# One tile's rounding ahead of another's copies, DRAM copies of x in three places, and the fourth group's tiles ahead of w1's maxima, in a fused FNet and MLP layer

## The chip, the core and the metric

The kernel runs on one core of a Trainium2 chip. The time is device microseconds from launch to end. Engines: TensorE (PE; PEld is its weight load), VectorE (DVE), ScalarE (ACT), GpSimd (POOL) and the queue of SyncE (SP), which issues most transfers. Each engine works through its own instructions in a fixed order.

## The reference

```python
def reference(A_x, A_dft_seq_re, A_dft_seq_im, A_dft_hid_re, A_dft_hid_im, B_x, B_w1, B_w2):
    ...
        a = jnp.einsum("bsd,ed->bse", x, dft_hid_re)
        b = jnp.einsum("bsd,ed->bse", x, dft_hid_im)
        y = jnp.einsum("ts,bse->bte", dft_seq_re, a) - jnp.einsum("ts,bse->bte", dft_seq_im, b)
    ...
        h = jnp.einsum("bsd,df->bsf", x, w1)
        h = jnp.maximum(h, zero)
        return jnp.einsum("bsf,fd->bsd", h, w2)
    x = A_x
    xn = _layernorm(x, axis=-1)
    return x + _A_ref(xn, A_dft_seq_re, A_dft_seq_im, A_dft_hid_re, A_dft_hid_im) + _B_ref(xn, B_w1, B_w2)
```

x is 2048 x 576, w1 is 576 x 4608, w2 is 4608 x 576, all float32. The result is x plus the real part of a two-sided Fourier transform of the normalized x plus a two-layer MLP of it.

## The kernel before

float32 products are made of float16 pairs: a value is scaled by a power of two and split into hi (ACT rounds it to float16) and lo (DVE takes the rest), and three matmuls, hi hi, hi lo and lo hi, make one product. The scales come from maxima over the weights: DVE's magnitude for w1 (max_w1), ACT's sum of absolute values for w2 (sum_w2), followed by a maximum over the partitions (power on POOL, or power_pe on PE and DVE in block 0, with its result in a tile named top).

x has 16 tiles of 128 rows, in four groups of four. stats takes the mean and the variance of a group's tiles on DVE and ends in r (the factor) and sh (the shift), four tiles at once. normalize (N) makes xn in float32 on DVE, or on ACT for tiles 10 and 11, and xs, the hi, on ACT. remainder (E) makes the lo, on POOL for tiles 1 to 11, on DVE for the others. transposes_dma (TD) lets POOL copy a piece and SP issue a DMA transpose into xT; the first four tiles are transposed by PE instead (transposes), and ACT copies them out of PSUM (copies).

The MLP runs in nine blocks b of 512 hidden columns. A step is a pair (b, g). mlp1 makes the four outputs of a step, each 128 hidden columns by the 512 rows of a group; mlp1_out applies the ReLU and makes h's hi and lo and four sums of them, from which mlp2 makes seven products by Strassen's scheme. Each product is 12 matmuls for a block of two. mlp2 has two PSUM tiles, so a product waits until the one two before it has been evicted: the first of an output by ACT (L583), the others by DVE (L586). In block 0 the results go into the acc tiles; POOL adds them to a DRAM tensor, spill, by a DMA that accumulates (L590). spill must hold x before that: copy_x(g) copies x of group g into it, DRAM to DRAM, by four transfers of 288 KB on SP.

At the start, stages are written out by hand, for tiles 0 to 11: that part runs from the loads of x to the first mlp2. Then a loop over the steps n runs mlp1 of step n and mlp2 of step n - 1. At n = 2 it also makes tiles 12 to 15 (the fourth group), while a list todo, emptied piece by piece by work(), prepares the weights of the next block: load_w1, max_w1, split_w1, then load_w2, sum_w2 and the splits of w2. w2's load for block 1 uses the two buffers named raw, so its second half waits until the second half of w1 is split.

The instructions of each engine are ordered by a scheduler. behind(key) and issue_after put what follows behind a named instruction of the same engine: "td" is the last transpose on SP, "add" the first eviction on DVE, ("sh", t) the last of a group's statistics, "pe" the last matmul of mlp2, "top" the maximum of power_pe. Where a key is not yet set, behind does nothing.

Of the kernel before, what the change touches and what calls it, by code (L numbers as in the profile page):

```python
# [13 lines left out]
AF = mybir.ActivationFunctionType  # L14
# [35 lines left out]
def kernel(  # L50
# [46 lines left out]

    def load_raw(key, src, shape):
        r = raws[key] = raw.tile(shape, F32, tag="raw", name="raw_" + "_".join(map(str, key)))
        order["raw"] = nc.sync.dma_start(r, src).ins  # L100

    def load_w1(b, i, parts=1):
        pool, tag = (raw, "raw") if b else (mlp, "stage")
# [4 lines left out]

    def load_w2(b, i):
        load_raw(("w2", b, i), w2[b, i], [P, 4, EH])  # L110
        if b == 1:
            copy_x(2 + i, "raw")


    def magnitude(dst, src):
# [82 lines left out]

        return tc.issue_after(order[key]) if key in order else nullcontext()

    def stats(ts, after=None):

        n = len(ts)
        mv = small.tile([P, n, 2], F32, tag=f"mv{n}", name=f"mv{ts[0]}")
        sts = [small.tile([P, 2, 6], F32, tag="st", name=f"st{t}", bufs=4) for t in ts]
        for t, st in zip(ts, sts):
            for j in range(2):
                with behind(after):
                    nc.vector.bn_stats(st[:, j, :], acc[t][:, j * EH : (j + 1) * EH])
                yield  # L210
        for i, st in enumerate(sts):
            order["stats"] = nc.vector.bn_aggr(mv[:, i], st.rearrange("p a b -> p (a b)")).ins
            yield
        r0, u, r, sh = (
            small.tile([P, n], F32, tag=f"{a}{n}", name=f"{a}_{ts[0]}") for a in ("r0", "u", "r", "sh")
        )
        m, v = mv[:, :, 0], mv[:, :, 1]
        stt = nc.vector.scalar_tensor_tensor
        order["root", ts[0]] = nc.scalar.activation(u, v, AF.Sqrt, bias=eps).ins
        nc.vector.reciprocal(r0, u)  # L220
        yield

        stt(u, v, EPS, r0, ALU.add, ALU.mult)
        yield
        nc.vector.tensor_tensor(u, u, r0, ALU.mult)
        yield
        nc.vector.tensor_scalar(u, u, -0.5 * SX, 1.5 * SX, ALU.mult, ALU.add)
        yield
        nc.vector.tensor_tensor(r, u, r0, ALU.mult)
        yield  # L230
        order["sh", ts[0]] = stt(sh, m, -1.0, r, ALU.mult, ALU.mult).ins
        for i, t in enumerate(ts):
            means[t], factors[t], shifts[t] = mv[:, i, 0:1], r[:, i : i + 1], sh[:, i : i + 1]

# [11 lines left out]
    def normalize(t, eng=nc.vector, after=None):  # L246
        stage = dbufs[t % 4]
        xn = xns[t] = stage[:, :D]

        xs = xss[t] = stage[:, D : 2 * D + P // 2].bitcast(F16)  # L250
        with behind(after):
            if eng is nc.scalar:
                nc.scalar.activation(xn, acc[t], AF.Identity, bias=shifts[t], scale=factors[t])
            else:
                eng.tensor_scalar(xn, acc[t], means[t], factors[t], ALU.subtract, ALU.mult)
            nc.scalar.activation(xs[:, :D], acc[t], AF.Identity, bias=shifts[t], scale=factors[t])

    def remainder(t, eng):
        xn, xs = xns[t], xss[t]
        eng.tensor_tensor(  # L260
            xs[:, D : D + REM], xn[:, KM * P :], xs[:, KM * P : D], ALU.subtract
        )
        eng.tensor_tensor(
            xs[:, D + REM : 2 * D], xn[:, : KM * P], xs[:, : KM * P], ALU.subtract
        )

    def transposes_dma(t, eng):

# [289 lines left out]
    def mlp2(b, g, n):  # L558

        qa, qb, first, row, col = PRODUCTS[n]
        if first:
            places[n] = ps2.tile([P, 2, 512], F32, tag="ps2", name=f"p2_{b}_{g}_{n}")[:, :, :EH]
        ps = places[PLACE[n]]
        for c in range(2):
            for i in range(NQ):
                h, w = hs[b, g, i], w2s[b, i]  # L570
                for j, (x, y) in enumerate(((0, 0), (0, 1), (1, 0))):
                    order["pe"] = nc.tensor.matmul(  # L572
                        ps[:, c], h[:, x, qa, c * P : (c + 1) * P], w[:, y, qb],
                        start=first and i == 0 and j == 0, stop=i == NQ - 1 and j == 2,
                        skip_group_check=not first,
                    ).ins
        if n in (0, 2, 3, 6):
            if b:
                o = sumbufs[sum_buffer(g, n)]
            else:  # L580
                o = accs[g].rearrange("p (h c) (j e) -> p h j c e", h=2, j=2)[:, row, col]
            sums[row, col] = o
            freed(nc.scalar.activation(o, ps, AF.Copy, scale=us[b]))  # L583
        else:
            o = sums[row, col]
            add = nc.vector.scalar_tensor_tensor(o, ps, us[b], o, ALU.mult, ALU.add)  # L586
            order["acc"] = order["vfree"] = add.ins
            order.setdefault("add", add.ins)
        if n not in (0, 2, 3):
            nc.gpsimd.dma_start(spill[g, row, col], o, accum_op=ALU.add)  # L590

# [2 lines left out]
    def max_w1(b, f):  # L594

        i, r = divmod(f, 2)
        if f == 0:
            mx["w1", b], sc["w1", b], pw["w1", b] = cell("mw1"), cell("sw1"), cell("pw1")
        if r == 0:
            mx["f", b] = cell("mf", 2)  # L600
        with behind("vfree" if b >= BB else "add" if b else ("sh", 1) if f > 1 else None):
            magnitude(mx["f", b][:, r : r + 1], raws["w1", b, i][:, r * KT : (r + 1) * KT])
        if r:
            if b:
                m = mx["w1", b][:, i : i + 1]
            else:
                m = mx["b", i] = small.tile([P, 1], BF16, tag=f"mb{i}", name=f"mb{b}_{i}")
            nc.vector.tensor_reduce(m, mx["f", b], AX.X, ALU.max)
# [39 lines left out]
        tt(a12, a12, a11, ALU.subtract)  # L648
        tt(r[:, 4], r[:, 4], r[:, 9], ALU.subtract)

    def sum_w2(b, i):

        if i == 0:
            mx["w2", b], sc["w2", b], pw["w2", b] = cell("mw2"), cell("tw2"), cell("pw2")
        if b:
            junk = mlp.tile([P, 5, GH], F32, tag="stage", name=f"j{b}_{i}")
            junk = junk.rearrange("p a b -> p (a b)")[:, : 4 * EH]
            junk = junk.rearrange("p (q e) -> p q e", e=EH)
        else:
            new_w2(b, i)  # L660
            junk = w2s[b, i][:, 0, :4]
        with behind("free" if b >= BB else None if b else ("root", 4)):
            nc.scalar.activation(
                junk, raws["w2", b, i], AF.Abs, scale=2.0**-10, accum_out=mx["w2", b][:, i : i + 1]
            )
# [72 lines left out]
    def prepare_w2(b):  # L738
        p = power_w2(b)
        steps = [long(lambda: sum_w2(b, 0))] + [lambda: None] * (b >= BB)  # L740
        steps += [
            long(lambda: (sum_w2(b, 1), b and next(p))),
            lambda: None,
            lambda: later(p) if b else next(p, None),
        ]
# [27 lines left out]
    for t in range(2 * TG, NT):  # L773
        load_x(t)

    def copy_x(g, key="td"):

        for row, col in itertools.product(range(2), range(2)):
            t = g * TG + row * 2
            src = x[t * P : (t + 2) * P, col * EH : (col + 1) * EH]  # L780
            with behind(key):
                nc.sync.dma_start(spill[g, row, col], src.rearrange("(c p) e -> p c e", p=P))

    warm = const.tile([P, 1], F32, name="warm")
    nc.scalar.activation(warm, eps, AF.Sqrt)

# [55 lines left out]
    tile_by(1, (3,), ps)  # L842
    weave(stats([4, 5, 6, 7]))
    copies(2, pt, ("root", 4))
    T(3)
    w = prepare_w2(0)
    w[0]()
    w[1]()
    tile_by(2, (0, 1, 2, 3), ps)
    for t in (4, 5, 6):  # L850
        N(t)
        E(t, GP)
        TD(t, GP)
    tile_by(3, (0, 1, 2, 3), ps)
    weave(stats([8, 9, 10, 11], ("sh", 4)))
    N(7, after=("root", 8))
    E(7, GP)
    TD(7, GP)
    w[3]()
    pq = ps2.tile([P, 2, 512], F32, tag="ps2", name="p1_0_1")  # L860
    qs = [pq[:, 0], pq[:, 1]]
    mlp1_out(0, 0, 0, *ps[:2], after="top")
    order["s0"] = order["s"]
    with behind("pm"):
        for t in (4, 5):
            tile_by(t, (0, 1), qs)
    for t in (8, 9):
        N(t, after="s4")
        E(t, GP)
        TD(t, GP)  # L870
    mlp1_out(0, 0, 1, *ps[2:])
    for t in (6, 7):
        tile_by(t, (0, 1), qs)
# [9 lines left out]
    for f in w[7:]:  # L883
        f()
    mlp1_out(0, 1, 1, *q2, after="w2")
    copy_x(0)
    mlp2(0, 0, 0)
    with behind("pe"):
        early = [mlp1(0, 2, 0), mlp1(0, 2, 1)]
# [102 lines left out]
    for n in range(2, len(steps)):  # L992
# [46 lines left out]
        for i in range(NF):  # L1039
            if n == 2:  # L1040
                ps.append(early.pop(0) if early else mlp1(b, g, i))
            else:
                mlp1_step(b, g, i, ps)
            if i % 2:
                mlp1_out(b, g, i // 2, *ps[i - 1 : i + 1], after="w2hi" if n == 2 else None)
            if i == (3 if n == 2 else 1):

                gates[n - 2] = order["s"], order["lo"]
            if n == 2:
                t = (g + 1) * TG + i  # L1050
                normalize(t)
                remainder(t, nc.vector)
                transposes_dma(t, nc.scalar)
                if i == 2:
                    todo += prepare_block(1)
                for _ in range(6):
                    work()
                continue
# [13 lines left out]
            if n > 3 and i % 2 and passes:  # L1072
                passes.pop(0)()
        if n == 2:
            copy_x(1)
            for q in range(7):
                mlp2(pb, pg, q)
    while todo:
# [229 lines left out]
```

## Time and profile before

| | us |
|---|---|
| median of three runs | 1260.19 (1258.29 to 1261.9) |
| the profiled execution | 1260.05, of which span 1258.3 |
| PE busy | 1231.6 |
| DVE busy | 1011.0 |
| ACT busy | 702.4 |
| POOL busy | 161.2 |

The granted TensorE clock of the profiled execution is 0.996 on average. In the profile a line such as L572 is a line of the kernel above. A row of the timeline shows the start, the length, engine, line, operation, output and inputs with their shapes, and how often in a row; the brackets hold the engine's idle time before it and what ended it. In a row of stretches, each engine's busy time is followed by its count of instructions.

### The profile page before, as it was taken

How to read it: one execution, taken by the hardware profiler on the slowest of the kernel's cores; microseconds unless marked ns; L12 is line 12 of the kernel's file. 1: busy time of each engine (PE TensorE's matmuls, PEld its weight loads, DVE VectorE, ACT ScalarE, POOL GpSimd, SP SyncE). 2: the span in 40 equal slices, each digit the busy share in tenths (PEclk: the TensorE clock that was granted, in tenths of full speed). 3: DMA queues.
4: the chain of work that ended last, by engine and by line, in shares of the span. 5: the costliest groups of instructions: out<-in, count | busy, mean ns of one | idle time of the engine just before them, and what ended most of it. 6: DMA issues, size and time to landing. Idle time of an engine off the chain costs nothing.

```text
span 1258.3 us, 25304 instructions
## 1 busy us (share of the span) xinstructions
PE 1231.6 (98%) x10269; PEld 983.0 (78%) x10269; DVE 1011.0 (80%) x1919; ACT 702.4 (56%) x1192; POOL 161.2 (13%) x207
## 2 busy tenths in 40 slices
PE   8888999999999999999999999999999999999998
PEld 7554656888888888888888888877777777777777
DVE  8997997878878787788788878556788888787885
ACT  5655466576676666676766756544553333333332
POOL 1521211111111111212121211100000000000000
PEclk9999999999999999999999999999999999999999
DMA  6787557565657575666666666640053435343420
GB/s 231 164 182 149 117 117 155 115 133 138 135 118 176 118 156 119 131 144 122 130 139 151 140 134 123 116 96 1 1 168 109 146 97 168 121 133 119 144 86 20
DMA packets 80901, 159.39 MB, mean 127 GB/s; under 512 B 22288, under 2 KB 41232, under 8 KB 80784
## 3 DMA queue, kind: packets, MB, share of 16 engines
q1 hardware_dynamic: 58000, 115.30, 28.6%
q0 software_dynamic: 22784, 42.48, 25.0%
q8 instruction: 80, 1.31, 0.5%
q14 instruction: 37, 0.30, 0.1%
HBM read 106.63 MB, written 51.90 MB: 126 GB/s over the span
## 4 chain that ended last, share of the span: by engine, by line
PE 78%; DVE 12%; ACT 1%; issue 1%; DMA 1%; POOL 0%; DVEq 0%; POOLq 0%; ACTq 0%
PE p L1240 26%; PE p L572 22%; PE bank L495 21%; PE pd L1121 8%; DVE w2s L186 2%; DMA raw_w<-in_w_dram 1%; PE p L339 1%; DVE dbuf L456 1%; DVE h L517 1%; DVE h L385 1%; DVE acc L441 1%; ACT w2s L185 0%; DVE sum L586 0%; DVE raw_w L697 0%; DVE dbuf L586 0%
## 5 line engine op out<-in xcount | busy, mean ns | idle before, releaser
L572 PE MATMUL p<-w2s,h 128*128 128x288 f16 x3024 | 410.0, 287 | 9.3 <-ACT acc L583 4.8
L572 PEld LDWEIGHTS <-h 128*128 128x128 f16 x3024 | 296.1, 98 | 86.6 <-issue 10.4
L1240 PE MATMUL p<-R,cs 128*128 128x288 f16 x2688 | 329.4, 286 | 0.0
L1240 PEld LDWEIGHTS <-cs 128*128 128x128 f16 x2688 | 263.0, 98 | 66.3
L185 ACT ACTIVATE cs<-c,sc_c 128x1024 f16<-128x1024 f32 x112 | 125.2, 1144 | 196.7 <-DVE c L1183 72.3
L186 DVE SCALAR_TENSOR_TENSOR cs<-c,sc_c,cs 128x1024 f16<-128x1024 f32 x112 | 141.0, 1282 | 54.7 <-ACT cs L185 54.7
L495 PEld LDWEIGHTS <-w1buf 128*128 128x128 f16 x1600 | 156.5, 98 | 22.8 <-issue 1.7
L495 PEld LDWEIGHTS <-dbuf 128*128 128x128 f16 x1200 | 117.4, 98 | 17.2 <-issue 1.5
L495 PE MATMUL bank<-xT,w1buf 128*128 128x256 f16 x832 | 109.8, 273 | 0.0
L1121 PE MATMUL pd<-dbuf,xT 128*128 128x288 f16 x832 | 103.8, 286 | 0.0
L495 PE MATMUL bank<-acc,w1buf 128*128 128x256 f16 x768 | 102.1, 273 | 1.0 <-DVE acc L525 0.9
L1121 PEld LDWEIGHTS <-xT 128*128 128x128 f16 x832 | 80.8, 98 | 22.0 <-issue 1.9
L517 DVE TENSOR_TENSOR h<-s,h 128x1024 f16<-128x1024 f32 x56 | 68.5, 1224 | 33.8 <-ACT h L514 33.6
L590 POOL DMA_DIRECT2D spill<-dbuf x70 | 61.0, 875 | 234.7 <-DVE dbuf L586 203.8
L502 ACT ACTIVATE h<-acc 128x256 f16<-128x256 f32 x112 | 45.9, 411 | 76.0 <-DVE acc L525 73.3
L495 PE MATMUL bank<-xT,dbuf 128*128 128x256 f16 x624 | 82.3, 273 | 0.0
L514 ACT ACTIVATE h<-s 128x1024 f16<-128x1024 f32 x56 | 59.1, 1056 | 34.5 <-DVE s L509 33.5
L495 PE MATMUL bank<-acc,dbuf 128*128 128x256 f16 x576 | 76.6, 273 | 0.9 <-DVE acc L525 0.9
L1246 DVE SCALAR_TENSOR_TENSOR o<-p,us_c,o 128x288 f32<-128x288 f32 x112 | 57.5, 514 | 12.6 <-PE p L1240 11.9
L984 ACT ACTIVATE f<-f 128x1024 f32<-128x1024 f32 x64 | 67.0, 1046 | 0.1
L503 DVE SCALAR_TENSOR_TENSOR h<-acc,h 128x256 f16<-128x256 f32 x112 | 47.3, 422 | 20.4 <-ACT h L502 20.4
L590 POOL DMA_DIRECT2D spill<-sum x42 | 36.3, 864 | 193.6 <-DVE sum L586 168.5
(161 smaller groups left out, 1537.3 us busy)
## 6 DMA issues: line engine op xcount, KB each, us to landing
spill<-dbuf POOLq DMA_DIRECT2D x70, 288.0 KB, 5.2
f<-in_cre_dram SPq DMA_DIRECT2D x32, 512.0 KB, 5.8
f<-in_cim_dram SPq DMA_DIRECT2D x32, 512.0 KB, 5.3
c<-in_cre_dram SPq DMA_DIRECT2D x32, 512.0 KB, 4.1
c<-in_cim_dram SPq DMA_DIRECT2D x32, 512.0 KB, 5.1
spill<-sum POOLq DMA_DIRECT2D x42, 288.0 KB, 4.9
raw_w<-in_w_dram SPq DMA_DIRECT2D x17, 640.0 KB, 6.0
raw_w<-in_w_dram SPq DMA_DIRECT2D x18, 576.0 KB, 5.0
```

Source lines behind the costliest of these rows:

```text
L185: nc.scalar.activation(hi, src, AF.Copy, scale=s).ins,
L186: nc.vector.scalar_tensor_tensor(lo, src, s, hi, ALU.mult, ALU.subtract).ins,
L495: nc.tensor.matmul(ps, l, r, start=first and m == 0, stop=m == len(todo) - 1, skip_group_check=not first,)
L503: stt(lo, src, 0.0, hi, ALU.max, ALU.subtract)
L514: order["s"] = nc.scalar.activation(hi_s, st[:, 1:], AF.Copy).ins
L517: order["lo"] = nc.vector.tensor_tensor(lo_s, st[:, 1:], hi_s, ALU.subtract).ins
L572: order["pe"] = nc.tensor.matmul(ps[:, c], h[:, x, qa, c * P : (c + 1) * P], w[:, y, qb], start=first and i == 0 and j == 0, stop=i == NQ ...
L590: nc.gpsimd.dma_start(spill[g, row, col], o, accum_op=ALU.add)
L984: nc.scalar.activation(f, f, AF.Abs, scale=2.0**-10, accum_out=sums_c[:, n, q : q + 1])
L1121: nc.tensor.matmul(ps[j], xT[g][:, kx, c * P : (c + 1) * P], dsp[j][:, hl, k], start=(t % 2 == 0 and n == 0), stop=(t % 2 == 1 and n == le ...
L1240: nc.tensor.matmul(ps, w[:, a, k], r[:, c, rq], start=first and k == 0 and j == 0, stop=k == HK - 1 and j == 2, skip_group_check=not first,)
L1246: order["o"] = nc.vector.scalar_tensor_tensor(o, ps, us["c"][:, n : n + 1], o, ALU.mult, ALU.add).ins
```

## The change

- copy_x of groups 0 and 1 is called just behind the loads of x, that of group 2 where group 0's was, and that of group 3 where group 1's was. load_w2 no longer issues copies for groups 2 and 3.
- Tile 4's normalize, remainder and transpose are written ahead of tile 3's copies, tile 5's ahead of the second sum over w2 (behind tile 5's hi on ACT).
- Tiles 6 and 7 come behind group 2's square root; the last two statistics of group 2 stand behind power_pe's maximum (the new argument late) and are woven in later; tile 8 follows them directly.
- In the loop's step n = 2, a tile of the fourth group is normalized, split and transposed ahead of the outputs of a pair (mlp1_out) instead of behind them.
- max_w1 of block 1 stands behind ("sh", 12), the fourth group's last statistic, instead of behind "add", the first eviction.
- The first output of step n = 3 (mlp1_step) stands behind the last matmul of mlp2.

```diff
     def load_w2(b, i):
         load_raw(("w2", b, i), w2[b, i], [P, 4, EH])
-        if b == 1:
-            copy_x(2 + i, "raw")
...
-    def stats(ts, after=None):
+    def stats(ts, after=None, late=None):
...
-        nc.vector.tensor_tensor(r, u, r0, ALU.mult)
+        with behind(late):
+            nc.vector.tensor_tensor(r, u, r0, ALU.mult)
         yield
-        order["sh", ts[0]] = stt(sh, m, -1.0, r, ALU.mult, ALU.mult).ins
+        with behind(late):
+            order["sh", ts[0]] = stt(sh, m, -1.0, r, ALU.mult, ALU.mult).ins
...
-            order.setdefault("add", add.ins)
...
-        with behind("vfree" if b >= BB else "add" if b else ("sh", 1) if f > 1 else None):
+        with behind("vfree" if b >= BB else ("sh", 12) if b else ("sh", 1) if f > 1 else None):
             magnitude(mx["f", b][:, r : r + 1], raws["w1", b, i][:, r * KT : (r + 1) * KT])
...
-    def copy_x(g, key="td"):
+    def copy_x(g):
...
-            with behind(key):
+            with behind("td"):
                 nc.sync.dma_start(spill[g, row, col], src.rearrange("(c p) e -> p c e", p=P))
 
+    copy_x(0)
+    copy_x(1)
...
     copies(2, pt, ("root", 4))
-    T(3)
     w = prepare_w2(0)
     w[0]()
-    w[1]()
+    N(4)
+    E(4, GP)
+    TD(4, GP)
+    copies(3, transposes(3), ("N", 4))
+    N(5)
+    E(5, GP)
+    TD(5, GP)
+    w[1](("N", 5))
     tile_by(2, (0, 1, 2, 3), ps)
-    for t in (4, 5, 6):
-        N(t)
+    tile_by(3, (0, 1, 2, 3), ps)
+    rest = stats([8, 9, 10, 11], ("sh", 4), "top")
+    for _ in range(3 * TG + 4):
+        next(rest)
+    for t in (6, 7):
+        N(t, after=("root", 8))
         E(t, GP)
         TD(t, GP)
-    tile_by(3, (0, 1, 2, 3), ps)
-    weave(stats([8, 9, 10, 11], ("sh", 4)))
-    N(7, after=("root", 8))
-    E(7, GP)
-    TD(7, GP)
     w[3]()
+    weave(rest)
+    N(8)
+    E(8, GP)
+    TD(8, GP)
...
-    for t in (8, 9):
-        N(t, after="s4")
-        E(t, GP)
-        TD(t, GP)
+    N(9, after="s4")
+    E(9, GP)
+    TD(9, GP)
...
-    copy_x(0)
+    copy_x(2)
...
-                mlp1_step(b, g, i, ps)
-            if i % 2:
-                mlp1_out(b, g, i // 2, *ps[i - 1 : i + 1], after="w2hi" if n == 2 else None)
-            if i == (3 if n == 2 else 1):
-
-                gates[n - 2] = order["s"], order["lo"]
+                with behind("pe" if n == 3 and i == 0 else None):
+                    mlp1_step(b, g, i, ps)
             if n == 2:
                 t = (g + 1) * TG + i
                 normalize(t)
                 remainder(t, nc.vector)
                 transposes_dma(t, nc.scalar)
+            if i % 2:
+                mlp1_out(b, g, i // 2, *ps[i - 1 : i + 1], after="w2hi" if n == 2 else None)
+            if i == (3 if n == 2 else 1):
+
+                gates[n - 2] = order["s"], order["lo"]
+            if n == 2:
                 if i == 2:
...
         if n == 2:
-            copy_x(1)
+            copy_x(3)
```

More of the change, by code (lines that the diff above doesn't have):

```diff
@@ L99, in load_raw @@
         r = raws[key] = raw.tile(shape, F32, tag="raw", name="raw_" + "_".join(map(str, key)))
-        order["raw"] = nc.sync.dma_start(r, src).ins
+        nc.sync.dma_start(r, src)
     def load_w1(b, i, parts=1):
@@ L255, in normalize @@
                 eng.tensor_scalar(xn, acc[t], means[t], factors[t], ALU.subtract, ALU.mult)
-            nc.scalar.activation(xs[:, :D], acc[t], AF.Identity, bias=shifts[t], scale=factors[t])
+            order["N", t] = nc.scalar.activation(
+                xs[:, :D], acc[t], AF.Identity, bias=shifts[t], scale=factors[t]
+            ).ins
     def remainder(t, eng):
@@ L262, in remainder @@
         )
-        eng.tensor_tensor(
+        order["E", t] = eng.tensor_tensor(
             xs[:, D + REM : 2 * D], xn[:, : KM * P], xs[:, : KM * P], ALU.subtract
-        )
+        ).ins
     def transposes_dma(t, eng):
@@ L649, in sums_w1, with sum_w2 @@
         tt(r[:, 4], r[:, 4], r[:, 9], ALU.subtract)
-    def sum_w2(b, i):
+    def sum_w2(b, i, after=("root", 4)):
         if i == 0:
@@ L661, in sum_w2 @@
             junk = w2s[b, i][:, 0, :4]
-        with behind("free" if b >= BB else None if b else ("root", 4)):
+        with behind("free" if b >= BB else None if b else after):
             nc.scalar.activation(
@@ L741, in prepare_w2 @@
         steps += [
-            long(lambda: (sum_w2(b, 1), b and next(p))),
+            long(lambda *a: (sum_w2(b, 1, *a), b and next(p))),
             lambda: None,
@@ L1042 @@
             else:
-                mlp1_step(b, g, i, ps)
+                with behind("pe" if n == 3 and i == 0 else None):
+                    mlp1_step(b, g, i, ps)
+            if n == 2:
+                t = (g + 1) * TG + i
+                normalize(t)
+                remainder(t, nc.vector)
+                transposes_dma(t, nc.scalar)
             if i % 2:
@@ L1049 @@
             if n == 2:
[L1050 to L1053, printed above, removed]
                 if i == 2:
```

## The prediction

> **What bounds the kernel now.** I read the page's busy line first, then stretches of the first 126 us, then TensorE's instructions in order of time, then the chain of waits.
>
> ```profile
> span 1258.3 us, 25304 instructions
> PE 1231.6 (98%) x10269; PEld 983.0 (78%) x10269; DVE 1011.0 (80%) x1919; ACT 702.4 (56%) x1192; POOL 161.2 (13%) x207
> ...
> 23.00:31.50 8.50, 8.15 (x146) 7.98 (x144) 7.96 (x28) 7.52 (x14) 3.73 (x6) 1.00 0.01 2
> 25.84:47.57 21.73, 18.70 (x249) 15.85 (x247) 21.52 (x52) 17.48 (x29) 15.92 (x23) 0.92 0.60 101
> 47.57:93.05 45.48, 39.61 (x261) 25.20 (x260) 44.42 (x101) 24.85 (x42) 11.20 (x12) 1.00 0.81 182
> 98.17:105.81 7.64, 5.28 (x34) 3.12 (x32) 0.00 (x1) 1.83 (x4) 0.36 (x1) 1.00 1.14 276
> 200.00:807.00 607.00, 604.52 (x5211) 509.57 (x5210) 483.88 (x1061) 406.68 (x797) 106.59 (x137) 1.00 0.65 135
> ```
>
> In the last five rows the columns are the stretch, its length, the busy time of PE, PEld, DVE, ACT and POOL, the granted clock, the DMA share and GB/s. The whole program leaves PE 1258.3 - 1231.6 = 26.7 us idle. From 200 to 807 us it loses 2.5 us in 607; there PE is the bound, and the change adds and removes no matmul. So whatever it is worth lies in the first 130 us or so. There DVE is the bound: busy 21.52 of 21.73 us and 44.42 of 45.48, up to the end of the split of w1's second half of block 1 at 93.05. Then DVE stands still for 7.64 us. DMA does nothing from 23 to 31.5 (share 0.01) and is full from 98 to 106 (1.14).
>
> TensorE in that time (start, length, instructions, and in brackets the idle time before and who ended it):
>
> ```profile
> 25.64 6.42 PE L339 MATMUL p<-xT,w1buf 128*128 128x128 f16 x112
> 35.16 0.16 PE L168 MATMUL pm<-top,ones 1*128 1x2 bf16 x1 [2.90 <-DVE top L165]
> 35.45 13.75 PE L339 MATMUL p<-xT,w1buf 128*128 128x128 f16 x140
> 49.04 1.63 PE L572 MATMUL p<-w2s,h 128*128 128x288 f16 x12
> 52.59 6.20 PE L339 MATMUL p<-xT,w1buf 128*128 128x512 f16 x28 [1.91 <-DMA xT<-dbuf]
> 58.62 8.98 PE L572 MATMUL p<-w2s,h 128*128 128x288 f16 x72
> 73.49 3.10 PE L572 MATMUL p<-w2s,h 128*128 128x288 f16 x24
> ...
> 91.16 3.10 PE L572 MATMUL p<-w2s,h 128*128 128x288 f16 x24
> ...
> 106.92 4.52 PE L572 MATMUL p<-w2s,h 128*128 128x288 f16 x24 [3.47 <-ACT acc L583]
> 115.25 1.02 PE L572 MATMUL p<-w2s,h 128*128 128x288 f16 x7 [1.00 <-DVE acc L586]
> ```
>
> At 91.16 the first output of group 3 is whole; from there PE runs 12.3 us without a gap, to 106.92 - 3.47 = 103.45. The gaps at 35, 52, 107 and 115 are the stalls that the change can reach. Only the last two stand behind the DVE-bound stretch; an earlier gap that closes buys nothing unless DVE also gets through its list sooner.
>
> **The wait at 107.** The chain of waits (start, length, what), the instructions of ACT and SP, and the page's DMA issues:
>
> ```profile
> 93.07 10.83 DMA raw_w<-in_w_dram
> 105.81 0.17 DVE half L126
> ...
> 103.98 1.16 ACT L663 ACTIVATE j<-raw_w 128x1152 f32<-128x1152 f32 x1 [7.57 <-DMA raw_w<-in_w_dram]
> 106.14 1.36 ACT L583 ACTIVATE acc<-p,c_ub 128x576 f32<-128x576 f32 x2
> 85.69 4.05 SPq L782 DMA_DIRECT2D spill<-in_x_dram  x4
> 93.45 4.07 SPq L782 DMA_DIRECT2D spill<-in_x_dram  x4
> raw_w<-in_w_dram SPq DMA_DIRECT2D x18, 576.0 KB, 5.0
> 106.44:109.85 3.41, 2.93 (x13) 1.87 (x13) 3.41 (x12) 1.30 (x3) 0.00 (x0) 0.50 0.18 62
> ```
>
> The second load of w2 of block 1 takes 10.83 us, against 5.0 for the median of 18 such loads. ACT stands in L663 (the sum over that load), and behind it on ACT waits the eviction L583 that PE needs; on DVE, L126 waits for POOL's maximum over that sum. Four copies of x leave SP just ahead of that load and four just behind it. After the gap the granted clock is 0.50 for 3.41 us: the 24 matmuls take 4.52 us instead of 3.10.
>
> **Part 1: the copies of x.** Sixteen copies of 288 KB stay sixteen. Groups 0 and 1 go behind the loads of x on SP and run from some 22.5 us, when DMA is idle. One stretch in which almost nothing but copies runs gives the rate:
>
> ```profile
> 54.00:56.00 2.00, 2.00 (x11) 0.88 (x9) 2.00 (x3) 1.05 (x2) 0.00 (x0) 1.00 0.83 251
> 31.79 18.62 SPq L277 DMA_TRANSPOSE xT<-dbuf  x8
> ```
>
> 8 x 288 KB = 2.36 MB at 251 GB/s is 9.4 us, so to about 32. Before, the first transpose left at 31.79, so DMA was free; now the transposes of tiles 4 and 5 share the queue with the last copies. This costs nothing as long as PE waits for L168 anyway; without that cover it is up to 2 us at 33. Group 2 takes the place of group 0, group 3 that of group 1, so around the two loads of w2 only group 3 is left, ahead of the first one. With eight copies (9.4 us of DMA) taken out of 85 to 106, the load should take about the 5.0 us of its median; the additions to spill that POOL issues are still there, so the bounds are 5.0 and 10.83. I take 5.0: landing at 98.1 instead of 103.9, 5.8 earlier. ACT's L663 and POOL then release DVE's L126 at about 100, which is when DVE gets there (93.05 to 98.17, and its list is unchanged); of DVE's 7.64 us some 2 remain. PE's gap of 3.47 goes, with it the slow clock (4.52 - 3.10 = 1.42), and the 1.00 at 115, since DVE's eviction moves with L126. Sum: -5.9 us, bounds -5.9 and 0. Next late is DVE: it has no more slack than these 2 us.
>
> **Part 2: the head (tile 4's hi, the maximum ahead of two statistics).**
>
> ```profile
> 28.92 2.39 ACT L256 ACTIVATE dbuf<-acc,sh,r 128x576 f16<-128x576 f32 x3
> 29.88 0.30 POOL L260 TENSOR_TENSOR dbuf<-dbuf 128x64 f16<-128x64 f32 x1 [4.77 <-ACT dbuf L256]
> 33.61 1.15 POOL L263 TENSOR_TENSOR dbuf<-dbuf 128x512 f16<-128x512 f32 x1
> 33.70 1.08 DVE L231 SCALAR_TENSOR_TENSOR sh<-mv,r 128x4 f32<-128x4 f32 x1
> 34.70 0.41 DVE L165 TENSOR_REDUCE top<-pm 1x2 bf16<-1x256 f32 x1
> 31.34:34.76 3.42, 0.92 (x15) 0.72 (x13) 3.25 (x9) 2.22 (x6) 3.42 (x7) 1.00 0.53 97
> ```
>
> ACT makes tile 4's hi ahead of tile 3's two copies and of the second sum over w2, so about 2.3 us sooner; POOL and the transpose follow. DVE takes top ahead of r and sh, which saves L231's 1.08 and r's short instruction, which I put at 0.2 to 0.3: PE's L168 moves from 35.16 to about 33.8. The clock is 0.92 over 25.84 to 47.57 because it halves after the gap; with 1.6 us of gap instead of 2.90 that may go. PE would be through its 140 matmuls at 46.3 instead of 49.04.
>
> That is not a gain yet. mlp2(0, 0, 0) also needs w2's first lo parts from DVE, and DVE now has r, sh, tile 8's xn and one subtraction of w2 ahead of them, four instructions more. I put its start between PE's 46.3 and the old 49.0. Then come the transposes of tiles 10 and 11: their hi stands on ACT behind w2's split and h's sums, which wait for DVE's scale. I get tile 11's xT, for which PE waited until 52.59, between 51 and 53.5. DVE's list is the same length, so at 57 it is where it was: I take 0 for the head, bounds -1.5 and +1.5.
>
> **Part 3: fourth group's tiles ahead of w1's maxima and of a pair's outputs.** DVE's 44.42 us from 47.57 to 93.05 stay what they are; only the order changes. Three rows show the order's price:
>
> ```profile
> 59.97 1.06 ACT L392 ACTIVATE h<-s 128x1024 f16<-128x1024 f32 x1 [3.52 <-DVE s L390]
> 60.30 0.82 DVE L586 SCALAR_TENSOR_TENSOR acc<-p,c_ub,acc 128x576 f32<-128x576 f32 x1 [0.36 <-PE p L572]
> 61.76 1.22 DVE L393 TENSOR_TENSOR h<-s,h 128x1024 f16<-128x1024 f32 x1
> ```
>
> Before, DVE evicts the second product (L586) and takes a maximum while ACT makes h's hi; now L393 stands ahead of L586 and the maxima wait for ("sh", 12). DVE then idles until ACT is done: 59.97 + 1.06 + 1.22 + 0.82 = 63.1 for L586's end instead of 61.1. PE's third set of 12 of the row at 58.62 (at 58.62 + 2 x 8.98 / 6 = 61.6) waits for that bank. The two sets ahead of it can run sooner than before, so PE idles there for some 3.5 us, and what follows is 63.1 - 61.6 = 1.5 later, less the 0.4 of two matmuls of the next step that now stand in the gap. The fourth group's transposes are out sooner, but mlp2(0, 1, .) is then paced by DVE's evictions behind the tiles' work and h's, and mlp1_step(0, 3, 0), put behind the pair's last matmul, follows only then. I get the first output of group 3 at 92.3 instead of 91.2: +1.1, the split of w1 and so the load's issue still at 93. Bounds: -1.5 (the transposes' lead of some 2 us carries through) and +3.
>
> **Sum**, against the profiled execution's 1260.05 us (span 1258.3 and 1.75 around it; the median of the runs is 1260.19): -5.9 + 0 + 1.1 = -4.8, so 1255.2.
>
> **Rivals.**
>
> *Clock.* PE's new gap ahead of the bank is 3.5 us. The clock halved after 31.34 to 34.76, with 0.92 us of work in it, and after the gap of 3.47 at 107. If it halves here too, 24 matmuls cost 1.4 more, and a second time while mlp2(0, 1, .) waits for its evictions, about 1.0: -4.8 + 2.4 = -2.4, so 1257.6. The Trainium skill (TensorE: Matmul & The Clock Gate, What's actually happening) has the clock fall only after a whole idle window of some 3.4 us in a free-running grid. By that rule a gap of this length would often pass, and the time is 1255.2; the row of 31.34 speaks against it, since that stretch was not idle throughout.
>
> *The load is no faster.* POOL's additions to spill run in the same time. If they, not the copies, hold the load, part 1 is worth nothing: +1.1, so 1261.2, or near 1260 with half of the effect of the copies ahead of the first load. Against it: the loads at other times have additions around them too and take 5.0.
>
> *Slower: POOL and DVE hold each other.* L231 takes 1.08 us beside POOL's L263 and ends with it, where L165, which reads PSUM, takes 0.41. Eight such POOL instructions (tiles 4 to 11) now meet another part of DVE's list: r, sh and w2's scale instead of statistics. At 1.15 each they can hold DVE 9.2 us; if about half of that did so before, 4.7 more. Tiles 10 and 11 and all behind slip by it, and with part 3's upper bound the first output of group 3 is 4.7 + 3 = 7.7 late. Part 1's 5.9 goes against that: +1.8. The gaps are then long enough for the clock to fall twice, 2.4 as above: +4.2, so 1264.3. It decides once that output is more than 5.9 late. The Trainium skill (SBUF — State Buffer, Who interferes with whom) says that whichever of the two starts first keeps the shared ports for its whole instruction. By that rule the order of starts, which the change shifts, decides each one; the trace agrees in the row of L231.
>
> *More.* The head's gain carries through (-1.5) and the transposes' lead too (-1.5 instead of +1.1): 1260.05 - 5.9 - 3.0 = 1251.2.
>
> **How the numbers follow.** Forecast 0.45; clock 0.2; load no faster 0.12; slower 0.13; more 0.10. 0.3% of 1260 is 3.8 us, about what a measurement of this kernel can tell from no change. Faster by more: the forecast without its upper tail (0.40) and "more" (0.10), 0.50. Within: the rest of the forecast, clock and load, 0.37. Slower: 0.13. The forecast's own range is 1253 to 1257.5; the range that holds 8 in 10 reaches "more" below and the load's case above: 1251 to 1261.5.
>
> **What would show it.** The load of w2 lands within 6 us of its issue, and PE has no gap at ACT's L583 near 100; DVE's idle time ahead of the scale of w2 is under 3 us instead of 7.6. L168 starts near 33.8. A new PE gap of 3 us or more stands near 60 to 63 and ends with DVE's eviction. DVE's end of the split of w1 is at 92 to 94.5. From 200 us on nothing differs. The prediction is wrong if that load still takes 9 us, if w1's split ends after 96, or if PE's gaps before 93 grow by more than 3 us.

## The result, and the profile after

| | before | after |
|---|---|---|
| median of five runs, us | 1260.19 (1258.29 to 1261.9) | 1254.26 (1254.06 to 1254.48) |
| profiled execution, us | 1260.05, span 1258.3 | 1254.06, span 1252.3 |

The ratio is 0.9953, 95% interval 0.9938 to 0.9967: 5.9 us less, against the 4.8 of the forecast and inside its range. The line numbers differ from kernel to kernel; in this one mlp1's matmuls are L341, mlp2's L574, ACT's eviction L585, DVE's L588, h's lo L395, the split L184, top L163, the sum over w2 L664.

The profiled executions don't start alike: the first matmuls of mlp1 stand at 11.50 us here, at 12.20 before and between 11.93 and 12.86 in the runs below. So the same work can stand up to 1.4 us apart in two profiles for that alone; "on before's scale" below means with that difference taken off.

The busy line of the changed kernel's page:

```profile
span 1252.3 us, 25300 instructions
PE 1229.2 (98%) x10269; PEld 980.5 (78%) x10269; DVE 1010.4 (81%) x1919; ACT 702.3 (56%) x1192; POOL 159.2 (13%) x207
```

1252.3 - 1229.2 leaves PE 23.1 us idle instead of 26.7: of the 6.0 us, 3.6 are idle time and 2.4 busy time. The profile has three stretches of 3.41 us at half the clock before and one now, and matmuls in such a stretch take longer. Stretches of the changed kernel (stretch, length, busy time of PE, PEld, DVE, ACT, POOL, granted clock, DMA share, GB/s):

```profile
47.57:93.05 45.48, 37.59 (x236) 23.76 (x237) 42.31 (x96) 24.12 (x41) 9.97 (x10) 0.96 0.86 177
98.17:105.81 7.64, 7.64 (x53) 5.01 (x52) 5.64 (x15) 4.58 (x7) 0.38 (x2) 1.00 0.33 45
130.00:200.00 70.00, 68.77 (x437) 41.43 (x435) 66.79 (x133) 44.33 (x76) 12.09 (x14) 1.00 0.60 124
200.00:807.00 607.00, 604.40 (x5220) 510.30 (x5219) 483.35 (x1061) 405.05 (x794) 108.01 (x138) 1.00 0.65 135
```

The last row is that of before within 0.1 us of PE's time, and behind it PE idles 3.4 us to the end (3.6 before): nothing differs from 200 us on. From 130 to 200 us PE is busy 68.77 us instead of 67.51, so 1.3 us of the gain lie behind the 130 us to which the prediction confined it. In the second row, which was the stall, PE is now busy all 7.64 us (5.28 before) and the DMA share is 0.33 instead of 1.14. The first row is worse than before: PE is busy 2 us less there, at a lower clock, and DVE, which was busy 44.42 us, now idles 3.2. TensorE in order of time shows where:

```profile
33.20 0.16 PE L166 MATMUL pm<-top,ones 1*128 1x2 bf16 x1 [1.64 <-DVE top L163]
33.29 12.47 PE L341 MATMUL p<-xT,w1buf 128*128 128x128 f16 x140
45.59 1.63 PE L574 MATMUL p<-w2s,h 128*128 128x288 f16 x12
49.47 6.20 PE L341 MATMUL p<-xT,w1buf 128*128 128x512 f16 x28 [2.25 <-DMA xT<-dbuf]
55.51 3.10 PE L574 MATMUL p<-w2s,h 128*128 128x288 f16 x24
...
61.44 7.71 PE L574 MATMUL p<-w2s,h 128*128 128x288 f16 x48 [2.39 <-DVE acc L588]
68.98 5.78 PE L341 MATMUL p<-xT,w1buf 128*128 128x512 f16 x26
...
91.77 3.10 PE L574 MATMUL p<-w2s,h 128*128 128x288 f16 x24
...
103.90 3.26 PE L574 MATMUL p<-w2s,h 128*128 128x288 f16 x24
...
110.76 1.63 PE L574 MATMUL p<-w2s,h 128*128 128x288 f16 x12 [0.79 <-DVE acc L588]
```

PE starts mlp2(0, 0, 0) at 45.59 instead of 49.04, 3.45 us ahead, and still leads by 58.62 - 55.51 = 3.1 at the next set. Then the new gap at 61 and a half clock behind it (48 matmuls take 7.71 us, where two runs of 24 take 2 x 3.10) eat the lead and more: the row at 68.98 was at 67.44. At 103.90 the gap of 3.47 is gone, and PE is 3.0 ahead again. Of each of these leads 0.7 is the earlier start.

The chain of waits and DVE's timeline of the changed kernel:

```profile
92.97 6.39 DMA raw_w<-in_w_dram
101.27 0.17 DVE half L124
```

```profile
59.43 1.22 DVE L395 TENSOR_TENSOR h<-s,h 128x1024 f16<-128x1024 f32 x1 [1.12 <-ACT h L394]
60.57 0.81 DVE L588 SCALAR_TENSOR_TENSOR acc<-p,c_ub,acc 128x576 f32<-128x576 f32 x1
...
91.26 1.68 DVE L184 SCALAR_TENSOR_TENSOR dbuf<-raw_w,c_sw,dbuf 128x640 f16<-128x640 f32 x2
...
101.27 0.17 DVE L124 TENSOR_SCALAR half<-top 128x2 f32<-128x2 f32 x1 [2.00 <-POOL top L121]
```

The load is issued at 92.97, where it was at 93.07 (w1's split ends at 91.26 + 1.68 = 92.94), and lands after 6.39 us instead of 10.83. DVE waits 2.00 us for the maximum over it. And DVE stands still for 1.12 us at 58 because h's lo, which must wait for ACT, is ahead of the eviction that PE needs; before, the eviction was first.

### The profile page after: what moved, and what is told of

The parts are those of the page before. It is cut to its first block, busy times and chain, and to the rows that moved or that the text cites. A ratio compares the mean times of both kernels' runs of the same rounds, so it can differ in the third digit from the quotient of the medians.

```text
span 1252.3 us, 25300 instructions
## 1 busy us (share of the span) xinstructions
PE 1229.2 (98%) x10269; PEld 980.5 (78%) x10269; DVE 1010.4 (81%) x1919; ACT 702.3 (56%) x1192; POOL 159.2 (13%) x207
## 4 chain that ended last, share of the span: by engine, by line
PE 78%; DVE 12%; ACT 2%; issue 2%; DMA 1%; POOL 0%; DVEq 0%; POOLq 0%; ACTq 0%
PE p L1253 26%; PE p L574 21%; PE bank L497 21%; PE pd L1134 8%; DVE w2s L184 2%; DMA raw_w<-in_w_dram 1%; PE p L341 1%; DVE dbuf L458 1%; DVE h L387 1%; DVE acc L443 1%; DVE h L519 1%; ACT w2s L183 1%; DVE dbuf L588 0%; DVE raw_w L698 0%; DVE raw_w L696 0%
## 5 line engine op out<-in xcount | busy, mean ns | idle before, releaser
L574 PE MATMUL p<-w2s,h 128*128 128x288 f16 x3024 | 410.4, 287 | 9.1 <-DVE acc L588 5.1
L574 PEld LDWEIGHTS <-h 128*128 128x128 f16 x3024 | 296.2, 98 | 86.4 <-issue 10.0
L184 DVE SCALAR_TENSOR_TENSOR cs<-c,sc_c,cs 128x1024 f16<-128x1024 f32 x112 | 141.0, 1282 | 54.4 <-ACT cs L183 54.4
L519 DVE TENSOR_TENSOR h<-s,h 128x1024 f16<-128x1024 f32 x56 | 68.5, 1223 | 33.9 <-ACT h L516 33.6
L585 ACT ACTIVATE dbuf<-p,c_ub 128x576 f32<-128x576 f32 x70 | 51.1, 732 | 16.5 <-PE p L574 16.2
```

The costliest lines, as they stand in the source:

```text
L184: nc.vector.scalar_tensor_tensor(lo, src, s, hi, ALU.mult, ALU.subtract).ins,
L519: order["lo"] = nc.vector.tensor_tensor(lo_s, st[:, 1:], hi_s, ALU.subtract).ins
L574: order["pe"] = nc.tensor.matmul(ps[:, c], h[:, x, qa, c * P : (c + 1) * P], w[:, y, qb], start=first and i == 0 and j == 0, stop=i == NQ ...
```

## The experiments

I call the three parts of the change the copies, the head and the group (part 3). Four kernels leave parts out. Times are medians; each ratio is to the kernel before run on the same chip (1259.25 to 1259.6 us, and 1260.19 for all three parts). The rows come from four chips, so rows are compared by their ratios.

| parts | us | ratio, 95% interval |
|---|---|---|
| copies | 1253.47 | 0.9954, 0.9940 to 0.9968 |
| head | 1256.65 | 0.9977, 0.9968 to 0.9986 |
| group | 1256.75 | 0.9977, 0.9968 to 0.9986 |
| copies, head | 1257.28 | 0.9979, 0.9970 to 0.9988 |
| copies, group | 1253.19 | 0.9950, 0.9938 to 0.9963 |
| head, group | 1254.98 | 0.9965, 0.9952 to 0.9978 |
| all three | 1254.26 | 0.9953, 0.9938 to 0.9967 |
| all three, lo behind the eviction | 1252.65 | 0.9945, 0.9932 to 0.9959 |
| copies, head, lo behind the eviction | 1252.13 | 0.9942, 0.9929 to 0.9954 |

The parts don't add: the three alone sum to 5.8 + 3.0 + 2.9 = 11.7 us, and together they give 5.9. The whole change (0.9953) is not set apart from the copies alone (0.9954).

**The copies alone** (the kernel before with)

```diff
-        if b == 1:
-            copy_x(2 + i, "raw")
...
+    copy_x(0)
+    copy_x(1)
     warm = const.tile([P, 1], F32, name="warm")
```

and groups 2 and 3 at the old places of 0 and 1.

> The kernel before with the copies of x alone moved (groups 0 and 1 behind the loads of x, 2 and 3 in the old places of 0 and 1). Theory (the copies carry the gain, 5 to 6 us, and the new order costs about 1): 1254 to 1255.5, the second load of w2 of block 1 lands within 6.5 us, DVE idles under 3 us ahead of w2's scale, no PE gap at ACT's eviction near 105. Rival (POOL's additions to spill hold that load, and the gain comes from the order of the engines' work): 1259 to 1261, and the load still takes 9 us or more.

1253.47, half a microsecond better than the theory's range. The chain of waits of this run:

```profile
94.80 5.56 DMA raw_w<-in_w_dram
```

The load takes 5.56 us, and PE's gaps from 93 to 126 us sum to 0.43 us instead of 4.83. The time has fallen by part 1's term of 5.9; the last pair of runs below shows that not all of it is this wait.

**The change without the copies** (copy_x of groups 0 to 3 back at the places of before).

> The changed kernel with the copies of x at their old places. Theory: 1260 to 1262, the load of w2 takes 9 us or more, PE has the gap of 3 us again, and DVE still ends the split of w1 at 92 to 94. Rival (order): 1254 to 1256.

1254.98: the theory missed, and the rival (order) has the time. The chain of waits and PE of this run:

```profile
93.19 7.20 DMA raw_w<-in_w_dram
```

```profile
106.56 1.63 PE L576 MATMUL p<-w2s,h 128*128 128x288 f16 x12 [0.20 <-ACT acc L587]
```

With all sixteen copies at their old places the load lands after 7.20 us instead of 10.83, and the gap at 107 is 0.20 us. What differs ahead of it is POOL's issue of the additions to spill; first the kernel before, then this run:

```profile
89.98 3.30 POOL L590 DMA_DIRECT2D spill<-acc  x3 [3.02 <-DMA spill<-in_x_dram]
```

```profile
85.89 1.11 POOL L594 DMA_DIRECT2D spill<-acc  x1 [1.16 <-DVE dbuf L456]
88.34 1.08 POOL L594 DMA_DIRECT2D spill<-acc  x1 [1.34 <-DVE half L126]
91.03 1.08 POOL L594 DMA_DIRECT2D spill<-acc  x1 [1.61 <-ACT acc L587]
```

Before, three additions leave in a bunch from 89.98 to 93.28, just ahead of the load at 93.07; the row puts their wait down to a copy of x. Here the outputs come sooner and the additions are spread. The bunch by itself does not slow the load: with the four copies ahead of the load moved away it stands there too, and the load takes 6.30 us (the last pair of runs below). Beside those copies it does go with the slow load: 10.83, 9.77 and 10.78 us with the bunch (before, the head alone, the copies behind moved), 7.20 and 7.55 without (here, the group alone). But in the last two the load is also issued 8.6 us behind the first of the four copies instead of some 7.5, so there was more time for the copies to drain. No run separates the two.

**The change without the group** (the loop of n = 2 and 3 and max_w1's key as before).

> The changed kernel without its third part: the fourth group's tiles behind a pair's outputs, w1's maxima behind the first eviction, the first output of step 3 not put behind mlp2. Theory (the order costs about 1, most of it the PE gap ahead of the bank at 61 and the slow clock behind it): 1252.5 to 1254, no PE gap of more than 1 us between 57 and 66. Rival (the fourth group's lead is what saves the stalls at 161 and 181 and more): 1255 to 1257.

1257.28: a miss, and 0.3 above the rival's range. DVE and then PE of this run:

```profile
60.04 1.23 DVE L395 TENSOR_TENSOR h<-s,h 128x1024 f16<-128x1024 f32 x1 [1.12 <-ACT h L394]
61.18 0.81 DVE L588 SCALAR_TENSOR_TENSOR acc<-p,c_ub,acc 128x576 f32<-128x576 f32 x1
```

```profile
62.04 7.60 PE L574 MATMUL p<-w2s,h 128*128 128x288 f16 x48 [2.38 <-DVE acc L588]
...
85.10 0.38 PE L341 MATMUL p<-xT,w1buf 128*128 128x512 f16 x1 [2.98 <-DVE dbuf L184]
```

The order lo, eviction and the gap behind it are there without part 3, which the forecast had made their cause. A second gap of 2.98 follows at 85, and w1's split ends at 93.95 + 1.68 = 95.6. The rival is right in this much: from 130 to 200 us PE idles 2.58 us here, 2.49 before and 1.23 with the whole change. The five kernels that have the whole group idle 1.1 to 1.2 us there, all others 1.5 to 2.6.

**The change without the head.**

> The changed kernel without its second part: tile 4's hi behind tile 3's copies, the maximum behind both statistics, tiles 6 to 8 as before. Theory (PE's 3 us at the head are waited away before DVE's evictions): 1253.5 to 1255.5. Rival (the head's 3.1 us carry through): 1257 to 1258.

1253.19, 0.3 below the theory's range; the rival missed. DVE's timeline of this run has the eviction first, and PE no gap there:

```profile
60.64 0.82 DVE L584 SCALAR_TENSOR_TENSOR acc<-p,c_ub,acc 128x576 f32<-128x576 f32 x1 [0.16 <-PE p L570]
61.60 1.23 DVE L391 TENSOR_TENSOR h<-s,h 128x1024 f16<-128x1024 f32 x1
```

Of all kernels here that keep mlp1_out whole, those with both copies and head have the lo ahead, and no others. Why the scheduler's order turns round just there is not shown.

**The lo behind the eviction**, in the changed kernel: the last line of mlp1_out becomes a function that is called later.

```diff
-    mlp1_out(0, 1, 1, *q2, after="w2")
+    lows = mlp1_out(0, 1, 1, *q2, after="w2", late=True)
...
     with behind("m1"):
         mlp2(0, 0, 1)
+    with behind("acc"):
+        lows()
```

> The changed kernel, with the lo of h's sums of the second group's second pair put behind DVE's first eviction of mlp2(0, 0, .) instead of ahead of it. Theory (the gap of 2.39 us at 61 and the half clock behind it are what the head costs): that eviction ends by 60.0 instead of 61.4, the gap falls under 1.2 us, the clock isn't halved at 62, and the time is 1252.5 to 1253.6, as low as without the head. Rival (DVE's list sets the pace up to the split of w1 at 93, so a gap of PE ahead of that buys nothing): the gap closes all the same, w1's split ends at 92.5 to 93.3 as now, and the time stays at 1254.0 to 1254.6.

1252.65, as the theory had it; the eviction ends at 60.7, which is 59.7 with the 1.0 us taken off by which this profile starts later than that of the changed kernel. PE of this run:

```profile
50.51 7.89 PE L341 MATMUL p<-xT,w1buf 128*128 128x512 f16 x28 [2.26 <-DMA xT<-dbuf]
58.24 8.98 PE L580 MATMUL p<-w2s,h 128*128 128x288 f16 x72
```

The gap at 61 is gone and 72 matmuls run through in 8.98 us. The load's issue moves from 92.97 to 91.78 in spite of that later start, so the rival (DVE's list alone sets the pace) doesn't hold. The clock fell all the same, at another gap (below). The two intervals overlap; the next use of the same edit is plainer.

**The same edit without the group** (copies and head; the same diff).

> The changed kernel without part 3 (the kernel of 1257.28 us), and again with the lo of h's sums behind DVE's first eviction of mlp2(0, 0, .). Theory (with copies and head together, that one order of two DVE instructions and the half clock behind its gap is most of what the head cost): gap at 62 under 0.8 us, w1's split ends by 94.5 instead of 95.6, time 1253.8 to 1255.6. Rival (the head costs by DVE's list before, not by that gap): the gap closes and the time stays at 1256.5 or more.

1252.13, better than expected and against 1257.28 without the edit; the ratios' intervals, 0.9929 to 0.9954 and 0.9970 to 0.9988, are apart. DVE and PE:

```profile
59.51 0.82 DVE L594 SCALAR_TENSOR_TENSOR acc<-p,c_ub,acc 128x576 f32<-128x576 f32 x1 [0.55 <-PE p L580]
60.24 1.22 DVE L397 TENSOR_TENSOR h<-s,h 128x1024 f16<-128x1024 f32 x1
```

```profile
57.84 8.98 PE L580 MATMUL p<-w2s,h 128*128 128x288 f16 x72
```

The swap of two DVE instructions is worth some 4.7 us here (0.9979 - 0.9942, of 1259): the gap at 62 is gone, in place of that of 2.98 at 85 stands one of 2.02 at 82, and w1's split ends at 93.8. It is the lowest time of all, though set apart neither from the row above it in the table nor from the copies alone, so with the order mended no gain of the group is seen.

**The head alone, the group alone** (the kernel before with one part).

> The kernel before with the head alone (tile 4's hi first, the maximum ahead of two statistics). Theory (the head only moves the stall from 50 to 61 and puts w1's split later, and the late load stays): gap of 2 us or more at 61 to 63, second load of w2 lands 8 us or more behind its issue, time 1260 to 1264. Rival (the head's 3.4 us of lead at 46 carries through): 1256 to 1258.

> The kernel before with the group's order alone (fourth group's tiles first, w1's maxima behind them). Theory (the order by itself takes away the stall at 107, since the outputs of group 1 and with them the additions to spill are spread and run sooner): load of w2 in 6.5 to 8 us, landed by 101, PE gap at ACT's eviction under 1 us, 1254 to 1256. Rival (the head's lead is needed for it): load 9 us or more, 1258 to 1261.

1256.65 and 1256.75. For the head the rival was right. Its chain of waits, PE and DVE (the eviction that before stands at 60.30, and the split of w1):

```profile
91.74 9.77 DMA raw_w<-in_w_dram
```

```profile
60.09 4.57 PE L576 MATMUL p<-w2s,h 128*128 128x288 f16 x36 [0.54 <-DVE acc L590]
...
105.52 1.94 PE L576 MATMUL p<-w2s,h 128*128 128x288 f16 x12 [4.04 <-ACT acc L587]
```

```profile
59.23 0.81 DVE L590 SCALAR_TENSOR_TENSOR acc<-p,c_ub,acc 128x576 f32<-128x576 f32 x1
...
90.04 1.68 DVE L186 SCALAR_TENSOR_TENSOR dbuf<-raw_w,c_sw,dbuf 128x640 f16<-128x640 f32 x2
```

Stretches from mlp1's first matmul to the start of that eviction, before and then of this run:

```profile
12.20:60.30 48.10, 41.26 (x462) 32.38 (x462) 46.59 (x123) 31.76 (x53) 21.62 (x30) 0.93 0.66 174
12.45:59.23 46.78, 41.02 (x471) 31.99 (x471) 45.73 (x123) 31.44 (x52) 19.49 (x30) 0.96 0.67 175
```

The load stays slow and the gap at 107 stays, but everything is earlier: w1's split ends at 91.7 instead of 93.05. DVE has 123 instructions up to the eviction in both kernels, but gets through them 1.3 us sooner: they take 0.9 us less, and it waits 0.5 us less. POOL's 30 instructions take 2.1 us less there; whether the two engines hold each other less in the new order is not isolated.

For the group alone:

```profile
95.01 7.55 DMA raw_w<-in_w_dram
```

The load takes 7.55 us, as its theory had it, but is issued only at 95.01, so it lands at 102.6 and not by 101, and the time missed the range by 0.75.

**A pair's outputs ahead of the tiles again**, the rest of the change kept.

```diff
+            if i % 2:
+                mlp1_out(b, g, i // 2, *ps[i - 1 : i + 1], after="w2hi" if n == 2 else None)
+            if i == (3 if n == 2 else 1):
+                gates[n - 2] = order["s"], order["lo"]
             if n == 2:
                 t = (g + 1) * TG + i
```

> The changed kernel with the outputs of a pair ahead of the fourth group's tiles again, as before; the maxima of w1 stay behind the last statistic and the first output of step 3 behind mlp2. Theory (the tiles' place in the loop is what part 3 gains with the head there): 1256 to 1257.6, as without all of part 3, with the gap of 2 us or more near 85 that ends at the remainder of a tile. Rival (the place of w1's maxima is what gains): 1254.0 to 1254.8.

1256.71 (ratio 0.9974, 0.9964 to 0.9984). PE of this run:

```profile
85.28 2.46 PE L574 MATMUL p<-w2s,h 128*128 128x288 f16 x12 [3.08 <-DVE acc L588]
```

The long gap near 85 is back, ended by DVE's eviction where the remainder of a tile was expected. So the tiles' place seems to be most of what part 3 gains behind the gap at 61: 0.9974 - 0.9953 of 1259 is 2.6 of 3.3 us. The share is rough: the runs of this kernel reach from 1253.96 to 1258.51, and the two intervals overlap.

**Only the copies between the two loads of w2; only those behind the second.** Twelve copies stay.

```diff
-        if b == 1:
-            copy_x(2 + i, "raw")
+        if b == 1 and i == 1:
+            copy_x(3, "raw")
...
+    copy_x(2)
     warm = const.tile([P, 1], F32, name="warm")
```

In the second kernel i == 0 keeps copy_x(2, "raw"), and copy_x(3) goes ahead.

> The kernel before with the four copies of group 2, which stood between the two loads of w2 and so ahead of the second, moved behind the loads of x; the other twelve stay. Theory (the second load waits for what was issued ahead of it): it lands 5.5 to 7.5 us behind its issue, the gap at 107 is under 1 us, time 1254 to 1256.5. Rival (it shares the engines with what stands behind it): 9 us or more, 1258.5 or more.

> The kernel before with the four copies of group 3, which stood just behind the second load of w2, moved behind the loads of x; the other twelve stay. Theory (the second load waits for what was issued ahead of it): it lands 9.5 us or more behind its issue, a gap of 2.5 us or more stays at 107, time 1258.5 to 1260.5. Rival (it shares the engines with what stands behind it): 5.5 to 8 us, 1254 to 1257.

1256.59 (0.9980, 0.9971 to 0.9989) and 1260.3 (1.0006, 0.9998 to 1.0015). The bunch of additions and the chain of waits with the copies between taken away, then the chain with those behind taken away:

```profile
89.96 3.30 POOL L590 DMA_DIRECT2D spill<-acc  x3 [1.87 <-DVE dbuf L455]
```

```profile
93.92 6.30 DMA raw_w<-in_w_dram
```

```profile
92.88 10.78 DMA raw_w<-in_w_dram
```

The load waits for the four copies issued ahead of it, and those behind it cost it nothing. In the first kernel the gap at 107 is gone, as expected; that of 115 stands at 111.56 with 1.52 us, and the time is 0.1 us above the range. The rows of this run would give 4.4 us (the gap of 3.47 and the slow clock's 1.42, less 0.52 more at 111), the medians give 2.5 (1.4 to 3.7 by the interval); why they differ is open. So with the load as fast as in the changed kernel the time falls by 2.5 us, and the other 3 us of part 1 come only when the other copies move as well. With the copies alone PE's gaps at 83 and 109 are shorter too (2.01 and 0.43 us, here 2.82 and 1.52); which of the other copies does that is not shown.

## Why the prediction was right, step by step

**The stall and its cure** (part 1) held: the load in 6.39 us (5.56 with the copies alone) for the forecast's 5.0, no gap at ACT's eviction, 2.00 of DVE's 7.64 us left, -5.8 for the copies alone against -5.9. The gap at 115 shrank to 0.79 (at 110.76) and did not go, and the load landed 1.3 us later than 98.1, 2.0 on before's scale. That -5.8 agrees so well is partly luck: the forecast drew nearly all of it from this one load, and with the load in 6.30 us and the gap at 107 gone the time falls by 2.5 us (4.4 by the rows) as long as the other copies stay. The rival in which POOL's additions hold the load is refuted by that same run, where the bunch of additions is still there; only beside the copies may the bunch add to the load's time.

**The head** was right in its start and wrong in its worth. L166 stands at 33.20, and since this run was already 0.70 us ahead at the row that before stands at 25.64, that is 33.9 for the forecast's 33.8. The 140 matmuls end at 33.29 + 12.47 = 45.8 (46.5 on before's scale; 46.3 expected); as the forecast allowed, the clock no longer halves at the wait ahead of them. But mlp2(0, 0, 0) starts at once, not up to 3 us later, and tile 11's xT is there at 49.47 (50.2 on before's scale), not at 51 to 53.5. The step that failed is "DVE's list is the same length, so at 57 it is where it was", with the 0 drawn from it. With the head alone the list has the same 123 instructions up to the first eviction, but DVE is through it 1.3 us sooner, w1's split ends 1.3 us sooner (1.6 on before's scale), and the time falls by 3.0 us, twice the bound of 1.5. Beside the copies the head costs 3.1 us instead (0.9954 to 0.9979), twice the bound on the other side.

**The gap at 60 to 63** came (2.39 us at 61.44, ended by DVE's eviction, against 3.5), but its cause was named wrongly. The text had L393 ahead of L586 because the maxima wait for ("sh", 12). The runs show that order with copies and head and without part 3, and not with part 3 and without the head. It comes with copies and head together, and the lo put behind the eviction takes their cost back (0.9979 to 0.9942).

**The group** was put at +1.1. With copies and no head it is about 0 (0.9954 and 0.9950), with the gap there it gains 3.3 (0.9979 to 0.9953), with the gap mended it is about 0 again, and alone it gains 2.9. About 1.3 us of PE's idle time go from 130 to 200 us, where the prediction did not look. w1's split ended at 92.94 and the first output of group 3 was whole at 91.77 (93.6 and 92.5 on before's scale), for 93 and 92.3.

So the sum of -4.8 came near the 5.9 by luck, through two errors of opposite sign: the head's cost beside the copies (3.1 against 0) was missed, and so was the group's gain behind it (3.3 against a cost of 1.1). The "clock" rival happened in half: the clock fell once behind that gap, as it said, not twice, and the lead of 2.4 us ahead of the gap (3.1 less the earlier start) paid for it. "More" comes nearer to what the head and the group bring alone (3.0 and 2.9), but beside the copies the two together bring nothing. No trace of the slower rival: POOL is busy 159.2 us, 2 less than before, and the first output of group 3 is 1.3 us late on before's scale, not the 5.9 from which that rival decides; with the head alone DVE's instructions even got shorter. Two of the signs that were to show the forecast right were narrowly missed: the load within 6 us (6.39) and the new gap of 3 us or more (2.39).

## What to carry to other kernels

When one transfer sits on the path, look at what was issued ahead of it on its queue in the same stretch; what stands behind it costs nothing here. A faster transfer is not yet the gain: here the load was just as fast in a kernel that gained less than half. Gains that end in the same wait don't add, so try each part alone and in pairs before judging it. Where an engine idles on another in front of an instruction that a third one needs (DVE's lo in front of an eviction), swapping the two can be worth more than the whole move around it.

## What the runs showed of the hardware

The granted clock halves behind a stretch that was not idle throughout, and whether a given gap does it depends on where a fixed grid of 3.41 us falls. In the kernel before, the stretches at half the clock start at 17.69, 34.76 and 106.44 us, 5 and 21 times 3.413 us apart. Stretches on that grid of the changed kernel, of the one with the lo behind the eviction, and of the kernel before:

```profile
45.43:48.85 3.42, 1.80 (x14) 1.12 (x12) 3.42 (x7) 1.46 (x4) 0.52 (x1) 1.00 0.73 137
48.85:52.26 3.41, 2.79 (x13) 1.30 (x14) 3.41 (x10) 2.66 (x6) 0.00 (x0) 1.00 0.89 255
59.10:62.50 3.40, 1.06 (x9) 0.86 (x9) 3.07 (x6) 0.93 (x2) 0.79 (x1) 1.00 0.22 90
62.50:65.90 3.40, 3.40 (x16) 2.07 (x15) 2.09 (x9) 1.04 (x2) 0.60 (x1) 0.50 0.72 89
```

```profile
47.38:50.80 3.42, 1.16 (x10) 0.66 (x8) 3.42 (x9) 2.29 (x5) 0.00 (x0) 1.00 0.72 140
50.80:54.22 3.42, 3.42 (x10) 1.24 (x9) 3.42 (x7) 2.76 (x4) 0.00 (x0) 0.50 0.90 290
```

```profile
14.28:17.69 3.41, 1.91 (x20) 1.27 (x18) 3.34 (x15) 1.05 (x2) 1.22 (x2) 1.00 1.03 405
```

The gap of 2.25 us ahead of 49.47 is split by the grid (PE busy 1.80 and 2.79 us of its two stretches) and costs no clock; nearly the same gap of 2.26 ahead of 50.51 falls into one stretch (1.16 busy), and the 28 matmuls behind it take 7.89 us instead of 6.20. The Trainium skill (TensorE: Matmul & The Clock Gate, What's actually happening) gives a free-running window of some 3.4 us, which these rows bear out, and has the clock fall after an idle window; here it fell after windows with 1.06 and 1.16 us of work in them. Where the threshold lies these rows don't show: a window with 1.80 us of work kept the clock, and behind that with 1.91 us (14.28 to 17.69, before) it was 0.50 up to 21.10. That early fall goes with no part of the change: the granted clock over 12 to 30 us is 0.91 before, with the copies alone, with the head alone and with head and group, and 1.00 with the group alone, the other two pairs and all three parts. So one such fall more or less can be chance.
